# Reordering the start of a fused attention and token/channel-mixing kernel: load order, row sums with the tokens as output rows, a 256-column second k^T v

## The chip, the cores and the metric

One core of a Trainium2 chip. The time is that of one execution on the device in microseconds (us); several executions of the kernel are timed and their median is taken. TensorE is PE (PEld its weight loads), VectorE DVE, ScalarE ACT, GpSimd POOL, SyncE SP.

## What is computed

Per head, with q, k, v of 8 batches x 8 heads x 576 tokens x 64 channels:

```python
kv  = einsum('bhsd,bhse->bhde', k, v)
out = einsum('bhsd,bhde->bhse', q, kv)
x   = out / sqrt(mean(out*out, -1) + 1e-06) * g_norm   # then heads side by side: (8, 576, 512)
a1  = alpha1 * x + beta1
u   = x + lam * einsum('ts,bsd->btd', w_tok, a1)
y   = u + lam * (relu((alpha2*u + beta2) @ w_ch1) @ w_ch2)
```

`w_tok` is 576 x 576, `w_ch1` 512 x 2048, `w_ch2` 2048 x 512. Inputs and output are float32; k^T v, q^T and the attention product run in a rounded float32 ("fp32r" in the profile), the mixing in bf16.

## The kernel before, in words

Every instruction is first recorded as an `Op` with engines it may run on and an assumed cost on each; `Prog.schedule` is a planner that steps through these costs, picks one engine and one PSUM bank for each operation and so writes one fixed in-order list for each engine. `synchronize` adds the semaphore waits, `emit` writes the program. The planner assumes that loads run one after the other: `dma_free` is the time when the first may begin, `dma_us` what each takes, and 2 us are added until it has landed. `pri` is a due time; `by_path` replaces it for everything on which batch 0's channel matmuls depend; a few lines at the end of the kernel (L1217 to L1226) shift groups of priorities by tag. `after` and `soft` order operations in the plan without a semaphore. `keep` is a number of PSUM banks that must stay free. Where the planner sees PE without work in the beginning it inserts dummy matmuls (`hot`, L1060).

Stages of a batch b, with their lines: load q, k, v (L521; the last 64 of 576 tokens apart, L529, the "tails"); cast them to fp32r (`round_in`, L414 on ACT and L415 on DVE); `kv` (k^T v, L594, 20 matmuls of 128 columns); `qtr` (q transposed by a matmul with an identity, L583, 128 columns); `norm` (q^T times kv, L583; square on ACT L651; sum on DVE L653; square root on ACT L656; reciprocal L659; `yn` L664, `rt` L666 on DVE; `xm` L669 on POOL); `tok` (25 matmuls L887 with the token weights `wt`, sums into `xm` L895, bf16 copy `ub`); `ut` (16 or 20 transposes L915, then `a2t` L924 on ACT or L926 on DVE); `ch1` (64 matmuls L957 of 512 columns, or 128 of 320 columns for a pair of batches; relu L942 on ACT, L943 on DVE, into `ht`); `ch2` (64 matmuls L977; sum into `xm` L985; store L988). The stages of batch b+1 and the loads of b+2 are woven into ch1 and ch2 of batch b. For an odd batch one ch1 covers 640 tokens with both tails.

Batch 0 is written apart (`first`) in two halves x = 0, 1 of four heads each: half loads, casts (`rounding`), `attend` (k^T v L713 with 256 columns, kv times g on L724, q^T L737 and L742, then the squared norms: products L756 and L769, squares on ACT L762 and L773, sums over channels by a matmul whose weights are a 0/1 matrix `sel` L781 so that heads become output rows, square root L788, five transposes L792 back to tokens, reciprocal L795; the products again with tokens as rows L807, scaled L815, times `e1` L822), and `mix` (token mixing L836, sums L846 and L854). `token_weights` casts `w_tok` with row sums (L1109, L1110), transposes it (L1134) and copies it to `wt`. Six staging buffers `st` take the big loads in turn: k, v, q of batch 0, four pieces of `w_ch1` (L1147; the fourth in k's buffer), q, k, v of batch 1 (v in the buffer of the first `w_ch1` piece, so its load waits for that piece's four casts), then four pieces of `w_ch2` (L1161). `w_ch2` is multiplied by lam while it is cast: of each piece one half on DVE, one on POOL (L1166).

All big loads are on SP's queue, in the order of their priorities:

```python
load_main("k", k, b, "SP", pri, (0,))   # then v, q of half 0, q's tail
load_main("k", k, b, "SP", pri, (1,))
load_main("v", v, b, "SP", pri, (1,))
load_main("q", q, b, "SP", pri, (1,))   # then w_tok, w_ch1 x4, q, k, v, tails of batch 1, w_ch2 x4
```

## Time and profile before

| | |
|---|---|
| median of 5 runs (lowest to highest) | 377.08 us (376.51 to 378.94) |
| the profiled execution: its time, its span | 377.29 us, 375.5 us |
| so outside the span | 1.79 us |
| PE busy / DVE / ACT / POOL | 361.6 / 225.7 / 176.4 / 86.2 us |
| mean granted PE clock | 0.985 |
| first ch1 matmul of batch 0 / of batch 1 (L957) | 35.16 us / 83.05 us |
| PE without work after 60 us | 1.1 us in all |

The span runs from the first to the last instruction. A line of the timeline gives start, length, engine, source line, operation, output and inputs, how many in a row, and in brackets the engine's idle time before it with what ended it. A group's mean is the length of one instruction, and neighbours on an engine overlap a little, so spacings are read from the timeline. A row of the windows view gives one stretch: its length, then for PE, PEld, DVE, ACT and POOL the busy time and the instructions, then the granted PE clock, the share of DMA time and GB/s.

### The profile page before, as it was taken

What the parts mean: (1) busy time and instruction counts of PE and PEld (TensorE: products, weight loads), DVE (VectorE), ACT (ScalarE), POOL (GpSimd) and SP (SyncE); (2) the same over time, 40 slices, a digit from 0 to 9 for tenths busy, and PEclk for the clock granted to TensorE, in tenths of its full rate; (3) what the DMA queues carried; (4) which work ended last, traced back from release to release, by engine and by line L of the source; (5) the groups of instructions that cost most, each with busy time, mean ns of one, the idle gap of its engine ahead of it and who ended that gap; (6) DMA issues with size and microseconds to landing.
All of it is one profiled execution on the core that took longest, in us unless ns stands there. A gap on an engine that the chain in (4) does not pass through costs nothing.

```text
span 375.5 us, 5601 instructions
## 1 busy us (share of the span) xinstructions
PE 361.6 (96%) x2258; PEld 224.9 (60%) x2258; DVE 225.7 (60%) x390; ACT 176.4 (47%) x310; POOL 86.2 (23%) x73
## 2 busy tenths in 40 slices
PE   7899799999999999999999999999999999999994
PEld 2687465569775564557865565557755544557641
DVE  4669669995995687539936694539534682520011
ACT  2489646666864266134741266135731274116400
POOL 4541087610430142003500123004400340000000
PEclk9699989999999999999999999999999999999999
DMA  7999999999959229211000110011000210020021
GB/s 191 327 352 360 265 382 312 296 285 311 324 133 301 78 58 308 56 58 56 2 2 28 58 56 0 2 56 58 0 2 28 85 29 1 30 84 2 0 84 56
DMA packets 47798, 47.99 MB, mean 128 GB/s; under 512 B 14097, under 2 KB 38681, under 8 KB 47773
## 3 DMA queue, kind: packets, MB, share of 16 engines
q1 hardware_dynamic: 47520, 47.47, 41.7%
q8 instruction: 17, 0.28, 0.3%
q10 hardware_dynamic: 252, 0.18, 0.2%
q14 instruction: 9, 0.07, 0.1%
HBM read 38.20 MB, written 9.44 MB: 127 GB/s over the span
## 4 chain that ended last, share of the span: by engine, by line
PE 84%; DVE 7%; DMA 5%; ACT 2%; issue 1%; SPq 0%; DVEq 0%
PE ps L977 33%; PE ps L957 29%; PE ps L887 10%; PE ps L583 4%; DMA st<-in_v_dram 3%; PE ps L594 2%; PE ps L915 2%; DMA st<-in_k_dram 2%; DVE w L1166 1%; DVE ht L943 1%; PE ps L713 1%; ACT w L414 1%; PE ps L737 1%; DVE yn L664 1%; DVE small L653 1%; PE ps L1060 1%
## 5 line engine op out<-in xcount | busy, mean ns | idle before, releaser
L957 PE MATMUL ps<-a2t,w 128*128 128x320 bf16 (+1 forms) x768 | 146.5, 332 | 1.1 <-ACT kvc L414 0.7
L977 PE MATMUL ps<-w,ht 128*128 128x512 bf16 x576 | 140.1, 381 | 0.1
L957 PEld LDWEIGHTS ps<-a2t,w 128*128 128x128 bf16 x768 | 73.6, 98 | 43.1 <-ACT kvc L414 1.2
L942 ACT ACTIVATE ht<-ps 128x640 bf16<-128x640 f32 (+1 forms) x105 | 68.0, 650 | 47.3 <-PE ps L957 46.9
L977 PEld LDWEIGHTS ps<-w,ht 128*128 128x128 bf16 x576 | 54.4, 98 | 59.2 <-DVE yn L664 0.6
L669 POOL TENSOR_TENSOR xm<-yn,g_bc 128x512 f32<-128x512 f32 x28 | 46.0, 1643 | 167.1 <-DVE yn L664 166.6
L985 DVE TENSOR_TENSOR xm<-ps,xm 128x512 f32<-128x512 f32 x32 | 22.0, 689 | 55.5 <-PE ps L977 55.0
L651 ACT ACTIVATE sq<-ps 128x512 f32<-128x512 f32 (+1 forms) x35 | 20.7, 591 | 49.0 <-PE ps L583 48.9
L895 DVE TENSOR_TENSOR xm<-ps,xm 128x512 f32<-128x512 f32 x28 | 19.3, 691 | 38.0 <-PE ps L887 36.8
L887 PE MATMUL ps<-rt,wt 128*128 128x512 bf16 x140 | 37.3, 381 | 0.0
L594 PE MATMUL ps<-vr,kr 128*128 128x128 f32 x112 | 34.8, 395 | 2.0 <-DVE ht L943 2.0
L583 PE MATMUL ps<-kvc,qt 128*128 128x128 f32 x112 | 33.2, 386 | 0.4 <-DVE ht L943 0.4
L583 PE MATMUL ps<-identr,qr 128*128 128x128 f32 x112 | 31.2, 374 | 0.7 <-DVE a2t L926 0.7
L924 ACT ACTIVATE a2t<-ps,cols 128x640 bf16<-128x640 bf16 (+1 forms) x15 | 11.7, 829 | 41.1 <-PE ps L915 41.1
L653 DVE TENSOR_REDUCE small<-sq 128x8 f32<-128x512 f32 (+1 forms) x35 | 23.6, 675 | 9.8 <-ACT sq L651 9.6
L594 PEld LDWEIGHTS ps<-vr,kr 128*128 128x128 f32 x112 | 23.3, 208 | 2.8 <-DVE ht L943 2.4
L664 DVE TENSOR_TENSOR yn<-ps,small 128x512 f32<-128x512 f32 (+1 forms) x35 | 24.0, 685 | 0.5
L666 DVE TENSOR_TENSOR rt<-yn,ge 128x512 bf16<-128x512 f32 x28 | 24.0, 856 | 0.5
L583 PEld LDWEIGHTS ps<-kvc,qt 128*128 128x128 f32 x112 | 22.3, 200 | 2.8 <-DVE ht L943 0.7
L583 PEld LDWEIGHTS ps<-identr,qr 128*128 128x128 f32 x112 | 22.0, 200 | 1.3 <-DVE a2t L926 0.9
L887 PEld LDWEIGHTS ps<-rt,wt 128*128 128x128 bf16 x140 | 13.5, 98 | 15.1
L414 ACT ACTIVATE qt<-ps 128x512 fp32r<-128x512 f32 (+1 forms) x29 | 15.8, 556 | 7.8 <-PE ps L583 6.7
(145 smaller groups left out, 375.2 us busy)
## 6 DMA issues: line engine op xcount, KB each, us to landing
st<-in_moe_w_ch_dram SPq DMA_DIRECT2D x8, 1024.0 KB, 11.9
out_dram<-xm SPq DMA_DIRECT2D x32, 256.0 KB, 2.3
st<-in_q_dram SPq DMA_DIRECT2D x7, 1024.0 KB, 7.8
st<-in_k_dram SPq DMA_DIRECT2D x7, 1024.0 KB, 10.0
st<-in_v_dram SPq DMA_DIRECT2D x7, 1024.0 KB, 12.1
ht<-in_moe_w_tok_dram SPq DMA_DIRECT2D x2, 576.0 KB, 9.1
kvft<-in_k_dram SPq DMA_DIRECT2D x8, 128.0 KB, 8.9
kvft<-in_v_dram SPq DMA_DIRECT2D x8, 128.0 KB, 7.4
```

What stands on the lines that cost most here:

```text
L583: P.op(F, lambda e, _: e.matmul(t.flat()[:, 128 * pr:128 * pr + 128], a(), m(), start=True, stop=True), r=r, w=[t], kind="F", **kw)
L594: return e.matmul(t.flat()[:, 128 * pr:128 * pr + 128], a, m, start=(c == 0), stop=(c == 4))
L651: P.op({"ACT": act_us(512)}, lambda e, _: e.activation(flat(sq[rows, s2]), t.flat(rows), ACT.Square), r=[t], w=[("sq", s2)], pri=p)
L653: P.op({"DVE": dve_us(512)}, lambda e, _: e.tensor_reduce(out=small[rows, s4], in_=sq[rows, s2], axis=AX.X, op=ALU.add), r=[("sq", s2)], w ...
L664: P.op({"DVE": dve_us(512)}, lambda e, _: e.tensor_tensor(out=hview(yn[rows, s3, :]), in0=hview(t.flat(rows)), in1=bc, op=ALU.mult), r=[t, ...
L666: P.op({"DVE": dve_us(512), "POOL": pool_us(512)}, lambda e, _: e.tensor_tensor(out=rto, in0=yn[rows, s3, :], in1=ge1[rows, :], op=ALU.mul ...
L669: P.op({"POOL": pool_us(512)}, lambda e, _: e.tensor_tensor(out=hview(x), in0=hview(yn[rows, s3, :]), in1=g_bc[rows, None, :].to_broadcast ...
L887: return e.matmul(t.flat(), wt[:, sc, col:col + 128], rt[:, sc, :] if sc < 4 else rtt[:], start=(sc == 0), stop=(sc == 4))
L942: return e.activation(dst, src(), ACT.Relu)
L957: return e.matmul(o, w1[:, dj, 128 * fj:128 * fj + 128], m, start=(dj == 0), stop=(dj == 3))
L977: P.op({"PE": 0.216}, lambda e, _: e.matmul(t.flat(), ht[:, fj, 128 * c:128 * c + 128], w2[:, fj, :], start=(fj == 0), stop=(fj == 15)), r ...
L985: P.op({"DVE": dve_us(512)}, lambda e, _: e.tensor_tensor(out=x, in0=t.flat(), in1=x, op=ALU.add), r=[t] + keys, w=keys, pri=p - 2)
```

## The change

Seven things are changed; all lie ahead of batch 1's channel matmuls, save that the two copies into `kvc` change in every batch. (1) The planner's loads begin at 3.4 instead of 1.2 us and take longer. (2) Of batch 0's second half q is loaded ahead of k and v. (3) The squared norms of batch 0 are summed with the squares as weights and `sel` (now 4 columns) as the moving operand: ten matmuls of 4 columns per half give tokens as rows at once; square root (20 elements) and reciprocal follow; the transposes and the 4 x 640 buffer go, and `sqtt` is filled up with zeros on POOL. (4) Priorities by tag: all of `wt` earlier, `kv.01`, `qtr.01`, `sums.01` earlier, `tok` of half 0 not; all `w_tok` transposes wait for all five casts, their copies are divided (three ACT, two DVE); one `w_tok` cast may go to DVE; half 1's first `rt` goes to POOL. (5) The casts of `w_ch1` are planned behind the last square root of batch 0 (`P.root`), the fourth piece on ACT or POOL. (6) `kv` of batch 1 uses 256 columns (the same 128 twice) in two PSUM tiles; the two copies into `kvc` of every batch no longer wait for each other. (7) `ut` of batch 0 puts two groups in one PSUM bank and all four `a2t` on DVE.

```diff
-        dma_free = 1.2
+        dma_free = 3.4
...
-                    w=STK(i) if x is None else [("st", i, x)], dma_us=2.8 if x is None else 1.4,
+                    w=STK(i) if x is None else [("st", i, x)], dma_us=3.0 if x is None else 1.5,
...
+                load_main("q", q, b, "SP", pri, (1,))
                 load_main("k", k, b, "SP", pri, (1,))
                 load_main("v", v, b, "SP", pri, (1,))
-                load_main("q", q, b, "SP", pri, (1,))
...
+            wide = b == 1
+            tiles = [P.ptile(1) for _ in range(2 if wide else 1)]
...
+                        if wide:
+                            o = tiles[pr // 2].flat()[:, 256 * (pr % 2):256 * (pr % 2) + 256]
+                            m = m[:, None].to_broadcast([128, 2, 2, DH])
...
+                    P.op(FW if wide else F, f,
...
+                apart[1].deps.discard(apart[0])
...
-                ts, tt = P.ptile(1), P.ptile(1)
-                for t, n in ((ts, 512), (tt, 64)):
...
-                            t.flat()[:, 0:n], sel[:, i, :],
-                            sqt[:, pr, :] if n == 512 else sqtt[:, pr, 0:64],
...
-                    P.op({"PE": 0.1}, lambda e, _, c=c: e.transpose(
-                        tt.flat()[:, 128 + 4 * c:132 + 4 * c], rs4[:, x, 128 * c:128 * c + 128],
...
+                ts = P.ptile(1)
+                for c in range(5):
                     for i in range(2):
...
+                        P.op({"PE": 0.12}, lambda e, _, c=c, i=i, pr=pr: e.matmul(
+                            ts.flat()[:, 4 * c:4 * c + 4],
+                            sqt[:, pr, 128 * c:128 * c + 128] if c < 4 else sqtt[:, pr, :],
+                            sel[:, i, :], start=(i == 0), stop=(i == 1)),
...
+                P.root = P.op({"ACT": 0.25}, lambda e, _, ro=ro: e.activation(
+                    ro, ts.flat()[:, 0:20], ACT.Sqrt, bias=eps[:], scale=1.0 / DH),
...
-                    P.op({"POOL": pool_us(256 * n)} if x == 0 else {"DVE": dve_us(256 * n)},
+                    P.op({"POOL": pool_us(256 * n)} if x == 0 or c0 == 0 else {"DVE": dve_us(256 * n)},
...
+            for djs in ((0, 1), (2, 3)) if b == 0 else ((0,), (1,), (2,), (3,)):
+                group(djs)
...
-                done.append(P.op({"ACT": act_us(S), "DVE": 0.48},
+                done.append(P.op({"ACT": act_us(S)} if sc % 2 == 0 else {"DVE": 0.48},
...
-                P.op({"ACT": act_us(512)} if qn < 3 else {"ACT": act_us(512), "DVE": dve_us(512, 2)}, f, r=STK(i),
-                     w=[("w1", qn, j)], pri=pri)
+                P.op({"ACT": act_us(512)} if qn < 3 else {"ACT": act_us(512), "POOL": pool_us(512, False)}, f,
+                     r=STK(i), w=[("w1", qn, j)], pri=pri).soft.add(P.root)
...
-            if o.pri < -500 and o.tag[-2:] == "00":
-                o.pri -= 3
+            if o.pri < -500 and o.tag[-2:] == "00" and o.tag[:3] != "tok":
+                o.pri -= 3 if "PE" not in o.cost else 0
...
-            if o.pri < -500 and o.tag == "sums.01":
-                o.pri -= 2
+            if o.pri < -500 and o.tag == "wt":
+                o.pri -= 4
+            if o.pri < -500 and o.tag in ("kv.01", "qtr.01", "sums.01"):
+                o.pri -= 6
```

## Prediction

> **What bounds the kernel now.** I read the page's slices first, then PE's timeline at the start of the channel matmuls, then the windows, then DVE's timeline.

> ```profile
> PE   7899799999999999999999999999999999999994
> PEclk9699989999999999999999999999999999999999
> ```

> From 60 us on PE is full (1.1 us of waits up to 375), and its work there is not changed: after batch 3 both programs give PE the same order. So the change is worth what it moves PE's position at 83 us, where batch 1's ch1 begins, and nothing that it gains earlier counts unless it is still there then. What holds PE before that:

> ```profile
> 42.67 1.26 PE L957 MATMUL ps<-a2t,w 128*128 128x512 bf16 x5
> 45.88 0.33 PE L594 MATMUL ps<-vr,kr 128*128 128x128 f32 x1 [1.96 <-DVE ht L943]
> ```

> ```profile
> 35.20:45.90 10.70, 7.59 (x51) 4.42 (x48) 7.58 (x19) 7.42 (x12) 0.00 (x0) 1.00 1.02 270
> 45.90:50.00 4.10, 4.10 (x17) 2.66 (x17) 2.90 (x4) 1.81 (x4) 1.63 (x1) 0.58 1.04 391
> 64.00:80.00 16.00, 16.00 (x99) 9.30 (x97) 15.05 (x25) 10.69 (x18) 7.50 (x5) 1.00 1.12 265
> ```

> ```profile
> 43.61 0.69 DVE L415 CAST vr<-st 128x1024 fp32r<-128x1024 f32 x1 [2.62 <-DMA st<-in_v_dram]
> 51.02 1.83 DVE L1166 TENSOR_TENSOR w<-st,lam_bc 128x1024 bf16<-128x1024 f32 x1 [1.48 <-DMA st<-in_moe_w_ch_dram]
> 55.58 3.01 DVE L1166 TENSOR_TENSOR w<-st,lam_bc 128x1024 bf16<-128x1024 f32 x1
> 71.92 1.65 DVE L666 TENSOR_TENSOR rtt<-yn,ge 64x512 bf16<-64x512 f32 x1
> ```

> Three things. PE stands 1.96 us because relus on DVE (L943) queue behind the cast of batch 1's v, which waits for its load until 43.61. Then PE runs at half clock (mean 0.58 up to 50; pairs of matmuls 0.56 instead of 0.29 us apart). And DVE is nearly full from 64 to 80 (15.05 of 16) and busy 34.65 of 39.4 us between 43.6 and 83: it is the next bound.

> **Part by part.**

> *Prologue to the first ch1 matmul (35.16 now).* No load is added, and SP issues the same bytes; of batch 0's second half q now lands third from last (14.8, where k landed), k at 16.4 and v at 17.8 in the places of v and q. Removed per half: four sum matmuls (L781), two roots (0.88 together), five transposes (0.47); from the first L781 of half 1 at 25.48 to the end of the reciprocal at 28.68 this is 3.2 us. Added: ten 4-column matmuls, not shown before, so between L792's 0.09 apiece (also 4 columns) and a 0.21 spacing (128-column fp32r back to back at L583, a heavier row): 0.9 to 2.1, I take 1.0, the row with the same columns; a root 0.30 (L656), a reciprocal 0.28. POOL gets two half casts (0.61 each), two zero fills (0.19 for one of 4x128) and one rt (1.33); DVE takes a w_tok cast from ACT. w_tok's last piece still lands near 22; five casts, then 25 transposes (1.6) and three ACT copies (0.6 each) end at 27.1, where token mixing may begin (29.26 now). Its 50 matmuls at 0.11 take 5.4, transposes 1.0; four a2t on DVE (0.54 each), only 0.4 of them beside PE's end, put the last at 35.2 and the first ch1 matmul at 33.7, 1.5 either way. The extra dummies (six more) run before k, v of half 0 are there: nothing, or up to 0.5.

> *The q gate.* That lead meets the next load. After's fifteenth ch1 matmul waits, with the transposes of q (batch 1), for a relu that stands on ACT behind the cast of q. q lands at 36.7 (k at 39.69 less 1 MB at 349 GB/s), cast 1.0, relu 0.6: PE goes on at 38.35, having stood about 1.6. Before, it restarted at 38.50 with 6 done; now 14.

> *The v gate.* v's load now waits for ACT's last cast of the first w_ch1 piece, which stands behind the root and 14 other ACT operations: 24.8 + 11 x 0.53 + 3 x 0.58 + 0.7 gives 32.6, where the issue came at 31.16. That costs nothing as long as the queue ahead (q and k, landing 36.7 and 39.7) is not empty: 7 us of cover; behind it on SP stand the tails and w_ch2, under the same cover. So v lands at 43.6 again, cast and relu end at 45.0, and there PE passes with 36 of ch1's 64 done, against 24 at 45.88: 0.88 + 12 x 0.216 = 3.5 ahead.

> *k^T v with 256 columns.* 20 x (0.118 spacing at L713, half 1, less 0.074, by which an L594 lengthens an L957 pair): -0.9. But the 20 come in one block: done at 48.9 (53.4 now), with norm behind them.

> *Clock.* The half clock from 46.5 to 49.9 cost 6 pairs x 0.27 = 1.6. Idle 1.56 us (6.67 to 8.22) and 1.96 us were each followed by 0.50; 1.14 us around 37 was not. The new waits are 1.6 at the q gate, 0.7 at the v gate: I take the gain of 1.6, with a loss of up to 1.0 left in the range.

> [...]

> So PE is 3.5 - 0.9 + 1.6 = **4.2 ahead** at 49. Now DVE. *Between 49 and 83* its work is the same in both (two qt casts and two relus fewer, two qr casts, a qtt and a ch2 sum more: +0.4), so what counts is its idle time and its waits for POOL. In the trace each DVE multiply of w_ch2 that starts while POOL runs its own half ends about 1.15 after POOL's: 1.23 alone, else 1.83, 3.01, 2.17; POOL's take 2.35 alone. After, POOL's chain begins first at 48.35, and DVE's four alternate with it: 50.65 to 51.8, 54.0 to 55.15, 57.35 to 58.5, 62.6 to 63.7; an xm (1.3) has come in between, before which one rt waits too. From 63.7 what remains of norm (four yn and four rt of 0.65, two sums, five reciprocals, a cast, a ch2 sum, one wait of 0.7 for POOL) ends the last rt at 72.4, against 73.57. PE, which needs at its 55th ch2 matmul the bank that yn of the last chunk frees (71.0), arrives at 67.7 and **stands 3.3 us**; the lead has gone into a new wait. After it PE has 34 large matmuls (7.3), 38 small ones (3.2) and 20 transposes (1.0): 82.6; DVE from 72.4 has 17 operations (9.9) and two short waits: 83.1 for the first ch1 matmul of batch 1 (83.05 now). A half clock behind the stall costs PE 0.8 to 1.7, of which DVE's bound hides 0.5: 0.7 on average. What is gained by then is that 17 small matmuls of batches 2 and 3, still to come before, are done: 17 x 0.074 = 1.26.

> *Rest.* The kvc copies side by side save up to 0.4 per batch on ACT, behind full PE: nothing; the one wait of 0.7 at 97 for kvc goes, I take half, 0.3. **Sum:** 1.26 - 0.05 - 0.7 + 0.3 = 0.8 to 0.9 less than the profiled execution's 377.29: **376.4** (against the median, 0.2 lower, 376.2).

> [...]

> **Rivals.**

> 1. *DVE does not cap it.* If DVE's multiplies slip between POOL's as the first did (1.23), four waits of about 1 vanish and the 4.2 of PE's lead stays: 373.1. For it: DVE idles 3.7 of its 15.5 us between 43.6 and 59.1 now. Against it: three of four did wait. Chance 0.22.
> 2. *Slower: rt behind POOL.* After moves norm forward into POOL's w_ch2 stretch (48.4 to 62.4; now norm's first rt starts at 63.17). If all five rt wait like the 1.65 row (+0.96 each) they cost 4.8, and the forecast's 0.9 becomes -3.9: 381.2; from 2.8 of added DVE time on it is slower by over 0.5%. Against it: only rt of chunk 0 is surely inside. Chance 0.10.
> 3. *The later v issue shows.* If the w_ch1 casts come so late that the queue runs dry (issue after about 38), v lands later one for one; 2 us late, the lead of 0.9 becomes -1.1: 378.4. Needs six us of error in ACT's order. Chance 0.06.

> **The numbers.** Forecast 0.62 (375.0 to 378.0, from the clock, 1.0, and DVE's waits, one POOL operation either way), rival 1 0.22, rival 2 0.10, rival 3 0.06. 0.5% (1.9 us) is about what a measurement of this kernel can tell from no change. Faster by more: rival 1 and 0.04 of the forecast; slower: rival 2 and 0.02 of the rest. The range 373.1 to 378.4 leaves out rival 2 and the far side of rival 1.

> **What would show it.** Right: first ch1 matmul near 34, PE waits ended by ACT's relu near 37 and DVE's near 44, L594's place in one block of 20 near 46 to 49, DVE without gaps from 52, PE waiting about 3 us for yn near 68 to 71, ch1 of batch 1 near 83 with norm of batch 2 begun. Wrong: no wait at 68 (rival 1), v landing after 44.5 (rival 3), rt of 1.4 and more (rival 2).

## The result: 0.6% slower, and the profile after

The changed kernel took 380.05 us (median of 22 runs, 376.66 to 382.15) against 377.28 us for the kernel before (41 runs, 375.46 to 379.55): a ratio of 1.006, 95% interval 1.0043 to 1.0078. The forecast was 376.4, with a range of 373.1 to 378.4. Runs more than 1.5% above their kernel's fastest are left out of its median and ratio (one of twelve in the repeat of the changed kernel, four of ten in the first kernel of the third set, one and two of twelve in the fifth set). The profiled execution took 379.69 us, span 377.6.

The same two rows of the page's slices (one digit for 9.4 us), now of the changed kernel:

```profile
PE   8799989899999999999999999999999999999994
PEclk9988999999999999999999999999999999999999
```

The half clock at the beginning of the row before is gone in this execution; a new one stands in the third and fourth slice, where before the clock was whole. Two rows of the windows (length; then busy time and instructions of PE, PEld, DVE, ACT, POOL; granted clock; DMA share; GB/s) show it:

```profile
21.77:25.18 3.41, 2.86 (x24) 2.42 (x23) 3.35 (x12) 2.31 (x8) 0.77 (x3) 1.00 1.05 409
25.18:32.01 6.83, 6.83 (x40) 5.55 (x40) 4.45 (x10) 5.71 (x11) 4.18 (x4) 0.50 1.06 395
```

PE is listed as busy for 2.86 of 3.41 us, and yet 6.83 us at a clock of 0.50 follow. What it was busy with, and what it then waited for, from PE's timeline:

```profile
23.05 0.27 PE L805 MATMUL ps<-sel,vr 128*128 128x4 f32 x1 [0.35 <-ACT vr L784]
23.53 0.94 PE L805 MATMUL ps<-sel,vr 128*128 128x4 f32 x7 [0.21 <-ACT vr L784]
24.34 0.36 PE L805 MATMUL ps<-sel,kr 128*128 128x4 f32 x2
...
37.43 3.43 PE L979 MATMUL ps<-a2t,w 128*128 128x512 bf16 x14
...
49.71 0.33 PE L582 MATMUL ps<-identr,qrt 128*128 128x128 f32 x1 [0.72 <-DVE qrt L415]
...
56.28 0.39 PE L979 MATMUL ps<-a2t,w 128*128 128x512 bf16 x1 [1.01 <-DVE ht L965]
...
73.36 0.33 PE L582 MATMUL ps<-identr,qr 128*128 128x128 f32 x1 [1.77 <-DVE yn L681]
...
85.75 0.31 PE L979 MATMUL ps<-a2t,w 128*128 128x320 bf16 x1
```

The new sums are ten matmuls that stream 4 columns each, 40 in all, where one of L979 streams 512: one alone has a record of 0.27. Batch 0's first ch1 matmul (L979) comes at 37.43 (35.16 before), batch 1's at 85.75 (83.05): 2.70 later, of which 0.6 comes back by the end (291.85 us of span are left there, 292.45 before), so the span is 2.1 longer. Between the two, PE stands 0.72, 1.01 and 1.77, in all 3.50; before it stood 0.43, 0.71, 1.96 and 0.38 there, in all 3.48. So 2.27 of the 2.70 are lost before the first ch1 matmul, and the waits behind it have moved but not grown. DVE's and POOL's timelines tell why PE waits now:

```profile
47.15 2.50 DVE L415 CAST qrt<-qft 64x512 fp32r<-64x512 f32 x1
...
52.08 3.42 DVE L1187 TENSOR_TENSOR w<-st,lam_bc 128x1024 bf16<-128x1024 f32 x1
55.53 0.69 DVE L965 TENSOR_SCALAR ht<-ps 128x512 bf16<-128x512 f32 x1
```

```profile
46.99 4.91 POOL L1187 TENSOR_TENSOR w<-st,lam_bc 128x1024 bf16<-128x1024 f32 x2 [9.21 <-DMA st<-in_moe_w_ch_dram]
52.06 2.36 POOL L1187 TENSOR_TENSOR w<-st,lam_bc 128x1024 bf16<-128x1024 f32 x1 [0.16 <-DMA st<-in_moe_w_ch_dram]
```

The cast of q's tail (0.42 in the kernel before, at 45.86) starts 0.16 after the first of POOL's two multiplies of w_ch2 (one line for both, 2.4 each) and ends at 49.65, 0.3 after that one; DVE's own multiply (1.21 and 1.22 for two without POOL's beside them, at 59.12 and 56.73) starts 0.02 after POOL's third and ends 1.08 after it. The relu behind it is the one that PE waits for at 56.28.

The mean granted clock of each run tells more: 15 of the 22 runs lie below 0.9865, their median is 380.23; the 7 above have 378.38. The slope of time over mean clock is 3.0 us for 0.01 in the changed kernel (3.3 in its repeat below), 0.4 to 0.7 in the kernel before (five sets of 17 to 35 runs, with much scatter). A drop of 0.01 is 7.5 us at half clock, so 3.75 us of PE's work: before, a fifth or less of that reached the end; after, most of it. A slope alone doesn't say which is the cause, since stands of PE come ahead of half clock too: in the kernel before, the 1.96 up to 45.88 and then 0.50 from 46.43 to 49.84.

### The profile page after: what moved, and what is told of

Same layout as the page of the kernel before. It is cut to its first block, busy times and chain, and to the rows that moved or that the text cites. A ratio compares the mean times of both kernels' runs of the same rounds, so it can differ in the third digit from the quotient of the medians.

```text
span 377.6 us, 5626 instructions
## 1 busy us (share of the span) xinstructions
PE 363.2 (96%) x2266; PEld 225.3 (60%) x2266; DVE 231.9 (61%) x396; ACT 169.4 (45%) x300; POOL 87.4 (23%) x78
## 4 chain that ended last, share of the span: by engine, by line
PE 82%; DVE 11%; DMA 2%; ACT 1%; POOL 1%; issue 1%; SPq 1%; POOLq 0%
PE ps L999 30%; PE ps L979 29%; PE ps L907 10%; PE ps L582 4%; DMA st<-in_v_dram 2%; DVE w L1187 2%; PE ps L600 2%; PE ps L937 2%; DVE rt L683 2%; PE ps L856 2%; DVE yn L681 1%; DVE small L670 1%; DVE ht L965 1%; PE ps L827 1%; PE ps L1155 1%
## 5 line engine op out<-in xcount | busy, mean ns | idle before, releaser
L979 PE MATMUL ps<-a2t,w 128*128 128x320 bf16 (+1 forms) x768 | 142.9, 329 | 2.8 <-DVE ht L965 1.5
L999 PE MATMUL ps<-w,ht 128*128 128x512 bf16 x576 | 138.4, 381 | 0.0
L979 PEld LDWEIGHTS ps<-a2t,w 128*128 128x128 bf16 x768 | 73.1, 98 | 45.7 <-DVE ht L965 2.1
L964 ACT ACTIVATE ht<-ps 128x512 bf16<-128x512 f32 (+1 forms) x107 | 69.4, 651 | 49.0 <-PE ps L979 48.5
L686 POOL TENSOR_TENSOR xm<-yn,g_bc 128x512 f32<-128x512 f32 x28 | 47.2, 1685 | 179.3 <-DVE yn L681 177.3
L915 DVE TENSOR_TENSOR xm<-ps,xm 128x512 f32<-128x512 f32 x28 | 19.3, 690 | 35.2 <-PE ps L907 34.1
L582 PE MATMUL ps<-identr,qr 128*128 128x128 f32 x112 | 32.3, 383 | 1.8 <-DVE yn L681 1.8
L600 PE MATMUL ps<-vr,kr 128*128 128x128 f32 (+1 forms) x112 | 31.1, 370 | 0.0
L683 DVE TENSOR_TENSOR rt<-yn,ge 128x512 bf16<-128x512 f32 x28 | 26.7, 955 | 0.4
L945 ACT ACTIVATE a2t<-ps,cols 128x640 bf16<-128x640 bf16 (+1 forms) x12 | 9.6, 843 | 31.8 <-PE ps L937 31.8
L600 PEld LDWEIGHTS ps<-vr,kr 128*128 128x128 f32 x112 | 21.8, 200 | 0.4
```

The source lines that it names most:

```text
L582: P.op(F, lambda e, _: e.matmul(t.flat()[:, 128 * pr:128 * pr + 128], a(), m(), start=True, stop=True), r=r, w=[t], kind="F", **kw)
L600: return e.matmul(o, a, m, start=(c == 0), stop=(c == 4))
L683: P.op({"DVE": dve_us(512), "POOL": pool_us(512)}, lambda e, _: e.tensor_tensor(out=rto, in0=yn[rows, s3, :], in1=ge1[rows, :], op=ALU.mul ...
L686: P.op({"POOL": pool_us(512)}, lambda e, _: e.tensor_tensor(out=hview(x), in0=hview(yn[rows, s3, :]), in1=g_bc[rows, None, :].to_broadcast ...
L964: return e.activation(dst, src(), ACT.Relu)
L979: return e.matmul(o, w1[:, dj, 128 * fj:128 * fj + 128], m, start=(dj == 0), stop=(dj == 3))
```

## Experiments

Two theories. **Clock**: half clock in the prologue, where PE is on the path, is the loss. **DVE**: DVE, held up by POOL's multiplies of w_ch2, sets when batch 1's norm ends, and the start matters little. What the expectations call the lock, or the shared resource, is what the last two timelines show: DVE's operation beside one of POOL's ends 0.3 to 1.08 after it. Line numbers shift by up to 40 in the edited kernels. Each "dummy" is a 512-column matmul on constants into the bank of the tile that the next matmul begins; it needs no data.

**First set.** The dummies, put in after planning, with every other order kept (tag, number of the tile, how many ahead of it):

```
FILL = {('qtr.01', 2): 3, ('kv.01', 0): 2, ('sums.01', 0): 2,
        ('sums.01', 3): 2, ('wt', 0): 1, ('x.01', 0): 1}
```

> The changed kernel (380.05 us, before 377.28) with eleven dummy matmuls of 512 columns put into PE's order between 16 and 27 us, nothing else moved. Clock theory: the loss is PE time at half clock between 25.4 and 32.0 us, which follows a stretch of 4-column matmuls and 128-column fp32r matmuls in which the array is little used; with the dummies the granted clock stays 1.00 there, the first ch1 matmul comes near 35 instead of 37.4, and the time falls by 2.2 to 3 to about 377.3. DVE theory: the start is not what decides, because DVE, held up by POOL's w_ch2 multiplies, sets when batch 1's norm ends; the clock stays up as well, but PE's waits at 50 to 56 and 71 to 73 us grow by what was won, and the time falls by 0.8 at most, to 379.2 or more.

Measured 377.86 (ratio to the kernel before 1.0016, 95% interval 1.0000 to 1.0032; so in brackets from here on): 2.2 less, the clock theory's lower edge. By the ratios (1.0060 and 1.0016) it is 1.7. Windows, then PE's timeline:

```profile
22.10:25.51 3.41, 3.19 (x33) 2.52 (x31) 2.80 (x11) 2.27 (x6) 1.90 (x4) 1.00 1.03 396
25.51:34.13 8.62, 8.48 (x86) 7.54 (x84) 7.54 (x18) 7.71 (x17) 5.75 (x9) 1.00 1.06 387
66.48:69.89 3.41, 0.80 (x5) 0.19 (x3) 3.30 (x6) 2.65 (x4) 1.26 (x1) 1.00 1.09 386
69.89:73.31 3.42, 3.41 (x13) 2.42 (x13) 3.30 (x5) 0.60 (x1) 1.27 (x1) 0.50 0.82 276
```

```profile
34.13 2.14 PE L998 MATMUL ps<-a2t,w 128*128 128x512 bf16 x8
...
69.90 0.47 PE L601 MATMUL ps<-identr,qr 128*128 128x128 f32 x1 [2.61 <-DVE yn L700]
...
83.88 0.31 PE L998 MATMUL ps<-a2t,w 128*128 128x320 bf16 x1
```

At whole clock the first ch1 matmul comes at 34.13, 3.3 earlier. But PE then waits 2.61 for yn, and a half clock follows that: of the 3.3, 1.87 is left at batch 1's ch1 (83.88 for 85.75).

The multiplies of w_ch2 replaced by plain casts, orders kept; this leaves lam out, so it shows only what the multiplies cost:

```diff
-  e.tensor_tensor(out=w2[...], in0=st[...], in1=lam_bc[...], op=ALU.mult)
+  copy_to(e, m, w2[...], st[...])
```

> The changed kernel with the eight multiplies of w_ch2 by lam (four on DVE, four on POOL) replaced by plain casts in the same places of the same orders: the multiplication by lam is left out. Clock theory: half clock at 25.4 to 32 stays, first ch1 matmul at 37.4 stays, PE's waits at 50 to 56 and 71 to 73 us (3.5 us in all) mostly go; the time falls by at most 1.5, to 378.5 or more. DVE theory: the fp32r cast of q's tail (2.50 us on DVE) falls to about 0.45, the first multiply (3.42) to 0.7, the waits go and with them 2.8 to 3.5 us: 376.6 to 377.3.

Measured 374.30 (0.9904, 0.9868 to 0.9939), 5.75 less than the changed kernel and more than either theory gave. The half clock of the prologue stands (24.24 to 31.07), the first ch1 matmul is at 36.53, and no wait of PE is left between 23 and 81 us; POOL's casts take 1.04 to 1.38 where its multiplies took 2.36 to 2.69, and DVE's cast of q's tail and its first operation on w_ch2 take 1.15 and 0.69 for 2.50 and 3.42. DVE's timeline:

```profile
46.26 1.15 DVE L415 CAST qrt<-qft 64x512 fp32r<-64x512 f32 x1
...
50.20 0.69 DVE L415 CAST w<-st 128x1024 bf16<-128x1024 f32 x1
```

Both edits together:

> The dummies of the first kernel of this call and the plain casts of the second (the multiplication of w_ch2 by lam is left out). Clock theory: about as the dummies alone, at most 1 lower, 376.3 to 377.3. DVE theory: about as the casts alone, 376.6, since the earlier start then meets the loads of batch 1. If the two causes add, each hiding part of the other, it is lower than either by 2 or more: 373.5 to 375.

374.22 (0.9918, 0.9893 to 0.9942): as the casts alone within its error, though the profiled execution, without any half clock, had a span of 370.1 against 372.5. In the medians, of six runs each, the two don't add: the dummies bring nothing here.

The old form of the sums taken back, the planner ordering anew:

```diff
-  ten of e.matmul(ts[:, 4 * c:4 * c + 4], sqt[...], sel[:, i, :])   # sel 4 wide
+  four of e.matmul(t[:, 0:n], sel[:, i, :], sqt[...])               # then two roots, five transposes
```

> The changed kernel with the sums of squares of batch 0 taken back to the old form (heads as rows: four matmuls of 512 and 64 columns, two roots, five transposes per half), the rest of the change kept; the planner orders the start anew. Clock theory: the array is busier in 18 to 25 us, no half clock there or a shorter one, and though the old chain is some 2 us longer the time is 377 to 378.5. DVE theory: whatever the start does, PE waits for yn near 71 us and the time stays at 379.5 to 380.5.

381.44 (1.0118, 1.0085 to 1.0152): both theories' ranges missed. There is no half clock near 25 (16 transposes of w_tok from 25.72 take 1.09, where 8 at half clock, from 24.43 in the kernel of plain casts, took 1.04), as the clock theory said, but the new plan has 7.7 us of waits of PE from 45 to 150 (1.70 for a relu at 45, 1.29 for rtt at 74, 1.43 for a relu at 104). Whole clock in the prologue alone doesn't make a fast kernel, and taking this part back is no cure.

**Second set.** The changed kernel again:

> The changed kernel unchanged, for a second profile on the same chip as the next three. Clock theory: half clock in at least one stretch again; its windows are 3.41 us long and lie differently against the kernel in each execution, so the stretch may begin anywhere from 22 to 26 us, and a second one may stand behind PE's wait at 71 to 73 us; time 378 to 382, runs with the lower mean clock (0.982) about 2 us longer than those with 0.990. If the half clock of the first profile was a chance, the mean clock is 0.997 or more and the time 377.

379.93 (1.0043, 1.0016 to 1.0070), mean clock of the profiled execution 0.983. It shows a second stretch of half clock, which by their mean clock most runs have, in another place than I expected. DVE, PE and the windows:

```profile
45.45 2.29 DVE L415 CAST vrt<-kvft 64x512 fp32r<-64x512 f32 x1
47.77 2.47 DVE L415 CAST qrt<-qft 64x512 fp32r<-64x512 f32 x1
```

```profile
47.80 0.39 PE L600 MATMUL ps<-vrt,krt 128*128 128x256 f32 x1 [0.77 <-DVE vrt L415]
50.30 0.33 PE L582 MATMUL ps<-identr,qrt 128*128 128x128 f32 x1 [1.53 <-DVE qrt L415]
```

```profile
48.32:51.73 3.41, 1.88 (x16) 1.68 (x16) 2.22 (x2) 0.65 (x2) 3.22 (x2) 1.00 1.05 400
51.73:55.15 3.42, 3.42 (x16) 2.63 (x15) 1.52 (x2) 0.69 (x3) 0.80 (x1) 0.50 1.09 387
```

POOL began at 45.10 here, before both tail casts; the second of its two multiplies ends at 49.96 and the cast of q's tail at 50.24. PE stood 0.77 and 1.53 for the two casts, and the clock is 0.50 from 51.73 to 55.15.

The other three kernels of the set start from the one with the dummies and move operations after planning: rt directly behind its yn; POOL's multiplies to DVE; both.

```python
seq.remove(o); seq.insert(seq.index(yn_of(o)) + 1, o)              # rt of batch 1
seq.remove(o); seq.insert(seq.index(sibling(o)) + 1, o); o.eng = "DVE"   # w_ch2
```

> The kernel with the dummies (377.86), and in batch 1's norm each rt on DVE put directly behind the yn that it reads, where before a reciprocal, a sum or a multiply of w_ch2 stood between and POOL's xm began first. DVE theory with the lock: the fourth and fifth rt take 0.69 instead of 1.63 and 1.14, the first 0.69 instead of 1.76 but the w_ch2 multiply behind it waits instead; DVE is 1.2 to 1.6 earlier at 70 us, PE's wait for yn falls from 2.61 to about 1.2 and less often leads to half clock: 376.0 to 377.0. Clock theory alone (DVE's waits do not decide once the start is at full clock): 377.5 to 378.2.

377.16 (1.0008, 0.9978 to 1.0038): between the two ranges. It is 0.7 below the median of the dummies alone, but the means of the twelve runs are 377.93 and 377.84, so no gain is shown. What held is the time of the fourth and fifth rt on DVE:

```profile
66.87 0.69 DVE L710 TENSOR_TENSOR rt<-yn,ge 128x512 bf16<-128x512 f32 x1
...
68.54 0.70 DVE L710 TENSOR_TENSOR rtt<-yn,ge 64x512 bf16<-64x512 f32 x1
```

> The kernel with the dummies (377.86), and POOL's four multiplies of w_ch2 put on DVE, each directly behind DVE's own of the same piece; POOL has only xm left. DVE theory with the lock: the eight take about 1.15 to 1.23 each, 9.2 to 9.8 in all, where the four took 9.37 with their waits; the relu behind the first comes 1 us earlier, PE's wait at 52 goes, and DVE is about as early at 70 us as before or 0.5 to 1 earlier: 376.6 to 377.8. If the waits were not a lock but DVE's own slowness on these operations, each of the eight takes 2 to 3 us, PE's wait at 70 grows by 4 or more, and the time goes to 381 or more.

379.90 (1.0046, 1.0021 to 1.0072). Seven of the eight multiplies take 1.21 to 1.23, as expected, and still it is slower, against my number: DVE has no less to do, and PE waits 3.68 for yn. DVE and PE:

```profile
50.14 2.36 DVE L1215 TENSOR_TENSOR w<-st,lam_bc 128x1024 bf16<-128x1024 f32 x2
```

```profile
72.28 0.48 PE L610 MATMUL ps<-identr,qr 128*128 128x128 f32 x1 [3.68 <-DVE yn L709]
```

> The dummies, rt directly behind its yn, and all multiplies of w_ch2 on DVE. DVE theory with the lock: no DVE operation in 45 to 72 us waits for POOL by more than 0.3, the last rt ends 2 to 3 us earlier than with the dummies alone (71.74), PE's wait for yn nearly goes and the half clock behind it: 374.5 to 376.0. Clock theory alone: 377.5 to 378.2.

379.04 (1.0029, 1.0006 to 1.0052): missed, for the same reason (a wait of 3.17 for yn at 70).

**Third set.** POOL's multiplies made to wait for the casts of the tails, in the changed kernel:

```diff
+  for o in w2_multiplies_on_POOL: o.deps.update(tail_casts_on_DVE)
```

> The changed kernel (380.05) with one thing altered: POOL's multiplies of w_ch2 wait for DVE's casts of the tails of v and q (batch 1), all orders kept. Lock theory: those casts took 2.29 and 2.47 us in the second profile of the changed kernel, each ending with an operation of POOL, PE stood 0.77 and 1.53 for them and fell to half clock behind it (51.97 to 55.38). With the wait they take 0.42, PE's stands at 48 to 50 go and so does that second stretch of half clock: the mean clock is 0.986 to 0.992 in nearly all runs, the time 378.0 to 378.8. If the casts were late for another reason (their loads), they still end at the same time and the time stays at 380.

378.64 (1.0015, 0.9980 to 1.0049): in the lock theory's range (over all ten runs 379.22, above it), and the interval holds no change against the kernel before as well. The casts take 0.42 and PE's waits at 48 to 50 are gone, as the theory said. Its forecast of the mean clock missed: two of ten runs lie in 0.986 to 0.992, the rest reach from 0.972 (383.59 us) to 0.998 (374.08 us). The prologue's half clock stands (26.37 to 33.20), and PE's wait for yn is 2.63, against 1.49 in the repeat. DVE, then PE:

```profile
47.24 0.42 DVE L428 CAST qrt<-qft 64x512 fp32r<-64x512 f32 x1
```

```profile
72.52 0.33 PE L595 MATMUL ps<-identr,qr 128*128 128x128 f32 x1 [2.63 <-DVE yn L694]
```

With dummies, rt behind yn and all multiplies on POOL (the edit above, the other way round):

> The kernel with the dummies and rt directly behind its yn (377.16), and DVE's four multiplies of w_ch2 put on POOL, each directly behind POOL's own of the same piece. DVE theory: DVE loses the 9.4 us of its four multiplies and gets back up to 5 waits of at most 2.4 behind POOL (about 5 in all); the last rt comes 3 to 4 us earlier, PE's wait for yn near 67 us (2.12) goes with the half clock behind it: 373.5 to 375.0. If POOL's eight multiplies (2.36 each alone, from 44.3 on) end too late for ch2, which needs the last piece near 65 us, PE waits there instead and the time is 377 or more.

377.60 (0.9997, 0.9981 to 1.0013): the second case. POOL is the cap, and PE waits for a piece of w_ch2:

```profile
68.24 0.39 PE L1031 MATMUL ps<-w,ht 128*128 128x512 bf16 x1 [2.04 <-POOL w L1219]
```

With dummies, and k^T v of batch 1 at 128 columns in place of the doubled 256:

```diff
-  o = tiles[pr // 2].flat()[:, 256 * (pr % 2):256 * (pr % 2) + 256]; m = m[:, None].to_broadcast([128, 2, 2, DH])
+  o = tiles[pr // 2].flat()[:, 256 * (pr % 2):256 * (pr % 2) + 128]
```

> The kernel with the dummies (377.86) with k^T v of batch 1 at 128 columns instead of the doubled 256, in the same places of the same order. Forecast's term for it: back to back a 128-column fp32r matmul takes 0.213 and a 256-column one 0.118, so ten in the block near 44 to 46 us cost 0.9 to 1.0 more and those between single transposes nothing; DVE's cap hides about half or all of it at 70 us: 377.8 to 378.8. If PE and not DVE decided, the whole 1.0 to 1.5 shows: 378.8 to 379.4.

376.95 (0.9989, 0.9962 to 1.0016): under both ranges. The block on PE, first of this kernel, then of the one with 256 columns:

```profile
44.15 0.86 PE L618 MATMUL ps<-vr,kr 128*128 128x128 f32 x5
44.84 0.28 PE L618 MATMUL ps<-vrt,krt 128*128 128x128 f32 x1
44.96 0.61 PE L618 MATMUL ps<-vr,kr 128*128 128x128 f32 x4
```

```profile
44.03 0.94 PE L619 MATMUL ps<-vr,kr 128*128 128x256 f32 x5
44.81 0.28 PE L619 MATMUL ps<-vrt,krt 128*128 128x256 f32 x1
44.93 0.64 PE L619 MATMUL ps<-vr,kr 128*128 128x256 f32 x4
```

From the block's start to its seventh matmul it is 0.81 with 128 columns and 0.90 with 256: in this place the 256 columns of the change's point (6) buy nothing.

With dummies, rt behind yn and POOL waiting for the casts of the tails:

> The dummies, rt directly behind its yn, and POOL's multiplies of w_ch2 waiting for the casts of the tails. Lock theory: as the first two alone (377.16) but without the runs at 380 to 382, in which I take the tail casts to have met POOL: median 376.3 to 377.0, highest under 379. If those runs have another cause, the spread stays and the median is 377.2.

378.21 (1.0010, 0.9988 to 1.0032). The highest run is 378.88 for 381.73 without the wait, as the lock theory said. The median is not lower: seven of twelve runs lie at 378.0 to 378.9, so those have another cause; its profile has a half clock behind a wait of 2.12 for yn. Against the first kernel of this set, which has neither dummies nor rt moved (1.0015), the two together gain nothing that is clear of noise.

**Fourth set.** Three of DVE's four multiplies on POOL, with dummies, 128 columns and rt behind yn; then three more dummies ahead of ('sums.01', 3) and ('wt', 0); then the kernel before with seven dummies ahead of its sixth ch1 group:

> The changed kernel with the eleven dummies, k^T v of batch 1 at 128 columns in place, rt directly behind its yn, and three of DVE's four multiplies of w_ch2 put on POOL (six on POOL, the two of the last piece divided as before). DVE's cap theory: DVE loses three multiplies (5.5 to 7 us with their waits) and gets waits of up to 2.3 in three rt; POOL ends the last piece near 63 to 65 us, about when ch2 needs it; PE's wait near 68 us falls from 2.1 to 2.6 to under 0.7, no half clock follows, the first ch1 matmul of batch 1 comes near 80.5 and the time is 374.5 to 375.8, faster than both kernels. If POOL then becomes the cap, as it did with all eight, PE waits for a w_ch2 tile or for yn and the time is 376.5 to 377.8.

377.50 (0.9995, 0.9964 to 1.0027): the second case. PE still waits 2.60 for yn at 70, and DVE's operations now end behind POOL's six multiplies in a row (15.31 from 43.78 on):

```profile
44.16 2.48 DVE L447 CAST qrt<-qft 64x512 fp32r<-64x512 f32 x1
...
54.38 2.49 DVE L714 TENSOR_TENSOR rt<-yn,ge 128x512 bf16<-128x512 f32 x1
```

> The kernel before it in this call with three more dummies between 22 and 25 us, where the array share of one 3.41 us window was 0.42 to 0.43 in the kernels with dummies. Clock theory: a window there still fell under the limit in some executions; with the three the runs at a mean clock of 0.989 or less go, each of the others is up to 0.6 longer, the median is within 0.5 of the kernel before it and the highest run 1 lower. If the remaining spread comes from elsewhere (POOL's hold on DVE, the loads), the spread stays and the median is 0.3 to 0.6 higher.

378.12 (1.0012, 0.9981 to 1.0042): the spread stays (four of twelve runs at 0.982 or 0.983); its profile has the clock falling at 48.41, behind a wait of 0.92 for the tail cast, not in the prologue.

> The kernel before the change with seven dummies of 512 columns put ahead of the sixth group of ch1 of batch 0, so that they fill 1.5 of the 1.96 us that PE stands before 45.88; nothing else moved. They keep the array share of the window before 46.4 near 0.7 and so the granted clock at 1.00 from 46.5 to 49.9. Forecast's step: this half clock cost PE 1.6 there. If PE's position at 49 us decides, the time falls by 1.2 to 1.6 to 375.7 to 376.1; if DVE's cap hides it (the last rt at 73.57, PE 1.1 us of waits later), it falls by at most 0.5, and the runs' time hangs less on their mean clock than in the changed kernel.

377.56 (0.9999, 0.9978 to 1.0019): no gain. In the profiled execution v came 1.3 later, PE still stood 2.16 and the clock fell at 48.07, so this execution doesn't test the step; but the twelve runs' mean clock rose (median 0.989 for 0.986) without the time following it. That agrees with the slopes: before the change, half clock costs little of the time (0.4 to 0.7 us for 0.01 of the mean clock).

**Fifth set.** rt behind yn and 128 columns together:

> The changed kernel with the eleven dummies, k^T v of batch 1 at 128 columns in place, and rt directly behind its yn, w_ch2 divided as in the change. If the gains of the last two add to that of the dummies (377.86, then 376.95 and 377.16 with one each): 376.2 to 376.8. If both meet the same cap (DVE and POOL on the w_ch2 multiplies), 376.8 to 377.6, no different from the kernel before.

376.84 (0.9987, 0.9959 to 1.0014): at the edge of the two cases. By the ratio it is no better than 128 columns alone (0.9989), so a sum of the two gains is not shown. Then w_ch2 in two steps, cast to bf16 on ACT and POOL and multiplied in place on DVE, without and with rt behind yn:

```diff
-  {"POOL" or "DVE"}: w2 = st * lam_bc
+  {"POOL" or "ACT"}: w2 = copy_to(st)      # to bf16
+  {"DVE": 0.62}:     w2 = w2 * lam_h       # lam in bf16
```

> The dummies, k^T v at 128 columns in place, and w_ch2 multiplied by lam in two steps: cast to bf16 on ACT (one half) and POOL (the other), then multiplied in place on DVE with lam in bf16, so that w_ch2 is rounded twice; the planner orders batch 1's stretch anew. POOL is left with casts of 1.04 (as in the kernel of plain casts). Theory of one shared resource: what DVE and POOL spend on w_ch2 falls from 4 x 1.15 + 4 x 2.36 = 14 us to 8 multiplies of 0.6 (if bf16 runs at twice the rate) or 1.15 plus 4 casts of 1.04 = 9 to 13.4. At 0.6 the cap lifts by some 3 to 4: 374.0 to 375.5, faster than both kernels. At 1.15 DVE is as full as now: 376.8 to 378.

> The kernel before it in this call with rt directly behind its yn. Shared resource theory with multiplies of 0.6: another 0.5 to 1 less where an rt waited for POOL, 373.5 to 375.0; with multiplies of 1.15: 376.3 to 377.8.

379.36 (1.0047, 1.0016 to 1.0078) and 381.66 (1.0071, 1.0036 to 1.0106): both missed. Four of the first's eight multiplies do take about half of 1.21 (two in 1.29, two in 1.28; the other pairs 2.36 and 2.05, with POOL at work beside them), but the new plan makes PE wait elsewhere; DVE, then PE, of the first:

```profile
51.42 1.29 DVE L1213 TENSOR_TENSOR w<-w,lam_h 128x1024 bf16<-128x1024 bf16 x2
```

```profile
106.90 0.31 PE L998 MATMUL ps<-a2t,w 128*128 128x320 bf16 x1 [2.28 <-ACT ht L983]
```

So it stays open whether shorter multiplies in the old order would lift the cap. Of all kernels that compute the whole, none is clear of the kernel before on the faster side.

## Why the forecast was wrong, step by step

- **Prologue.** First ch1 matmul: forecast 33.7, measured 37.43 with half clock from 25.18 to 32.01, and 34.13 with the dummies. The sum's parts held within 0.5 (token mixing forecast at 27.1 begins at 27.47 there); the missing term is the clock. The step that failed is *Clock*: it asked only how long PE stands ("the new waits are 1.6 at the q gate, 0.7 at the v gate"), took a running PE for a safe one, and put the clock of the prologue at nothing without a reason. The token-major sums replace 1152 streamed columns per half by 40 and a series of weight loads; PE is listed as busy for 2.86 of the 3.41 us from 21.77, and by the last section's estimate the array streams columns in 0.29 of them. An estimate with the same working: 1112 columns at 0.42 ns are 0.47 us, 0.14 of 3.41 us; with them the share would have been about 0.43, and 0.42 is the lowest that was followed by whole clock in the profiles of the kernels before and after. With the dummies, which keep it, the time is 2.2 less, of the 3.65 by which the forecast missed; the other 1.45 stays with whole clock in the prologue.
- **q and v gates.** Neither happened. v was issued at 35.97 (forecast 32.6, though the terms given there add up to 33.1) and the queue did run dry (98 and 26 GB/s at 35 to 37 us): rival 3's event. But q and k had landed by then, DVE cast v at 44.77 without waiting for it, and k^T v began without a wait at 47.33, and at 44.03 with the dummies (forecast 45.0). So that event was not the loss.
- **k^T v with 256 columns.** Forecast 0.9 of the lead lost, 0.118 a matmul in a block against 0.074 between ch1 matmuls. The spacing held (0.12), but 128 columns in a block take 0.112: the loss belongs to the block and not to the columns, and only ten of the twenty came in one block. The spacing of 0.21 that the prologue's range and the expectation for 128 columns use isn't in L583's rows: back to back they start 0.11 to 0.17 apart, 0.25 once; 0.21 is the spacing of L827's 128 columns at half clock (from 28.92 to 29.35 in the changed kernel).
- **Half clock at 46 to 50.** Gone in the first profile, as forecast, but back at 51.7 in the second; and the seven dummies in the kernel before give no sign that it cost anything there, where the forecast counted a gain of 1.6. The 0.7 that the sum takes for a half clock behind the stand at 68 is an estimate of mine; with the dummies one of 3.42 us did follow the wait of 2.61 (69.89 to 73.31).
- **DVE as the cap.** Right with the dummies, and so is the place: forecast a stand of 3.3 for yn at 67.7 to 71.0 and ch1 of batch 1 at 83.1; with the dummies it is 2.61 at 67.3 to 69.9 and 83.88. Undersized were DVE's waits for POOL: I priced them for multiplies and rt, not for the fp32r casts of the tails (0.42 becomes 2.29 to 2.50), which PE waits for directly (0.72 at 49.71; 0.77 and 1.53 in the repeat).
- **The 17 small matmuls done early.** Forecast 1.26 less after 83 us; measured 0.6. Of the 0.66 that are missing, 0.43 are PE's waits between 86 and 151, which grew from 1.07 to 1.50; the rest is open.
- **The slower rival** (rt behind POOL, 381.2) came near the time by another road: three of five rt took 1.15 to 1.75, 2.5 over their 0.69 in all. That the time lies near this rival's is luck: with the dummies the time falls though nothing was done for rt.

The shares don't add to a sum. Shown are 2.2 for the prologue's clock in the changed kernel as it stands, and 5.75 for leaving out the multiplies of w_ch2. With the multiplies left out the dummies gained nothing (374.22 for 374.30), and no kernel that computes the whole came clear of the one before; what each cause is worth with the other gone is not settled.

## What to carry to other kernels

Before turning a wide matmul into narrow ones on a path that PE carries, count the columns that are left to stream and look at the granted clock behind them, not only at PE's busy time: here a window of 3.41 us with PE busy for 2.86 was followed by 6.83 us at 0.50. A few dummies without data can be cheaper than the clock (2.2 less in the changed kernel), though they aren't free (eleven at 0.216 are 2.4 us of PE). And where DVE's operations lengthen beside POOL's, as the fp32r casts of the tails did from 0.42 to 2.29 and 2.50, plan the two engines' operations as if they shared a queue: in this kernel, moving them from one engine to the other moved the wait and didn't end it.

## What was not expected of the hardware

For each such window of the profiles before and after I estimated the share of it in which the array streams columns: 512 columns are 0.216 us by the ch1 rows, so 0.42 ns a column, put at the middle of each matmul's record and weighted by the rows used of 128. Of 210 windows at whole clock (up to 6 us before a program's end) three were followed by half clock. By the estimate their shares are 0.07, 0.29 and 0.29; the lowest share that was followed by whole clock is 0.42, the next 0.44. With the columns put at the start or the end of the records, the highest of the three is 0.31 and the lowest of the others 0.40. The window at 48.32 of the repeat, at about 0.38 by its rows, was followed by half clock too. The limit of which an expectation of the fourth set speaks is my estimate from such shares; no run was made to find it.

PE's busy share doesn't part these windows. The one at 21.77 of the changed kernel was busy for 84% (estimated share 0.29), the one at 48.32 of its repeat for 55% (0.38), those at 5.47 and 43.02 of the kernel before for 54% and 43% (0.07 and 0.29), and half clock followed all four; the one at 69.56 of the changed kernel was busy for 60% (0.55), and the clock stayed whole.

So in these profiles PE need not be idle for a window ahead of half clock: it was busy for 2.86 of 3.41 us ahead of the fall at 25.18. Runs of one kernel differ in their mean clock (0.979 to 0.992 in the 22 of the changed kernel). That a stretch shorter than two windows fills a whole one in some executions and not in others would explain it; this is my guess, and no run shows it.
